# A fused sketch attention and tanh layer: the first batch's keys by groups, its products spread over more engines, and a newly searched order

## The chip, the cores and the metric

The kernel runs on one core of a Trainium2 chip. Its time is the device time of one execution in microseconds, and the median of several runs is what counts. The core has five engines with a queue of instructions each, which they take strictly in order: TensorE (PE in the profile, with its weight loads as PEld), VectorE (DVE), ScalarE (ACT), GpSimd (POOL) and SyncE (SP), which here only issues transfers. Engines wait for each other through semaphores. Work is in SBUF (128 partitions) and in PSUM (eight banks, where matmuls put their results).

## What is computed

Two stages behind each other. The first is attention with a polynomial sketch: keys and queries go through two small matrices S1 and S2, the two results are multiplied with each other in all 8 x 8 pairs, and attention is linear in these 64 products. The second adds a wide layer whose activation is h - tanh(h).

```python
# q, k, v: (4 batches, 4 heads, 1088 rows, 32); S1, S2: (8, 32)
def phi(x):
    a = einsum('rd,bhsd->bhsr', S1, x)
    b = einsum('rd,bhsd->bhsr', S2, x)
    return einsum('bhsi,bhsj->bhsij', a, b).reshape(..., 64)
q_p, k_p = phi(q), phi(k)
kv  = einsum('bhsf,bhsd->bhfd', k_p, v)
z   = sum(k_p, axis=2)
num = einsum('bhsf,bhfd->bhsd', q_p, kv)
den = einsum('bhsf,bhf->bhs', q_p, z)[..., None] + 1e-06
x   = (num / den) as (4352 tokens, 128)
h   = x @ w_in                # w_in: (128, 2048)
out = (h - tanh(h)) @ w_out   # w_out: (2048, 128)
```

The kernel splits the last line: x @ (w_in @ w_out) is done with one folded 128 x 128 matrix, and tanh(-h) @ w_out is added.

## The kernel before

The tokens are handled as four batches of 1088 rows, each of nine tiles of 128 (the last is half full). A batch's attention goes through these steps, named here as in the code:

- **kT**: the raw keys are turned on DVE in blocks of 32 x 32 (L595 in the first batch, L591 later). **kproj** (L604): PE projects them with the sketches (psk). **kab** (L612): DVE turns the projections back, into the two factors a and b per key.
- **gram** (L620): PE adds up a times b over all keys, which gives z. **zm** (L625), **ufold** (L629) and **uw** (L632) fold z into w4, the matrix that projects the queries.
- **qT** (L762), **qproj** (L774), **qab** (L782): the queries' turn, projection with w4, and turn back; the product with z comes out with them.
- **wk** (L652): the 64 products per key. In the first batch ACT first copies a part of kab into PSUM (**ka**, L641), so that DVE reads one operand there. **tiles** (L665, **sums** L734 in later batches): PE multiplies wk with v. **kvs**, **fold0** and **kvb** bring the result into the form that the numerators use.
- **dm**, **den**, **rden**, **qa** (L801 to L810): the denominator, its reciprocal, and the query factor divided by it. **qp** (L685, L820 later): the 64 products per query. In the first batch PE turns them (**qt0**, L700) and ACT or DVE copies them back (**qpB**, L707); in later batches DVE turns them (qpT, L826).
- **num** (L716, L843 later) and **x** (L722): the numerators, which are x.

The second stage goes through ten windows of tokens: 256, 256, seven of 512, and 256. A window has 16 matmuls of **L1** (L952, one for each block of 128 hidden columns), the **tanh** on ACT (L956), 16 of **L2** (L973), and two of **lin** (L937) with the folded matrix in two bf16 parts, whi and wlo. L1 writes two pairs of PSUM banks in turn, L2 and lin add in one bank; DVE turns the result (osb, L989) and SP writes it out. The last window multiplies the other way about (L968). Ahead of the dense part w_in and w_out are cast to bf16 (L872, L876), w_in is transposed on PE in four steps (**turn**, L886; copied by w_inT, L891), and **wfold** (L898) multiplies the two matrices.

The order of all this is not the code's. Each step is recorded as an operation with an engine, a cost, what it reads and writes, and a priority; ORDER lists for each engine the operations' numbers in the order in which they are issued, found by a search ahead of time, and PLACES gives for some steps another engine than the code names. Semaphore waits are worked out from the recorded reads and writes. Where PE would have nothing to do in the opening, matmuls of a tile of zeros (wz, L531 and L532) are put in; how many is worked out from the planner's costs.

The opening's queues before the change are these. SP issues k (three transfers: 160 columns of each of four groups, 128 of three groups, 64 of the last), q's first 512 columns, v (four), w_in and w_out, with the rest of q between. DVE turns the keys in two parts (five tiles, then four), then does kab of five tiles, qT, kab of four, qT, one wk, zm, a wk, uw, two wk, qab (two), dm, den, rden, qa (two of each), and four qp. POOL does wk of the first five tiles, then casts weights. PE does kproj in two parts, gram, ufold, qproj, tiles, fold0, qt0 of tiles 0 and 1 with two of w_in's transposes between, qt0 of tiles 2 and 3, the numerators, the third transpose, and then L1.

Of the kernel before, what the change touches and what calls it, by code (L numbers as in the profile page):

```python
# [13 lines left out]
R = 8  # L14
# [4 lines left out]
NT = 9  # L19
# [3 lines left out]
FB = 0  # L23
# [7 lines left out]
COLD = 6800  # L31
EARLY = 5000
CHUNK = 256
HEAD = 56
# [19 lines left out]
    ),  # L54
    "scalar": (
# [4 lines left out]
    ),  # L60
    "vector": (
# [5 lines left out]
    ),  # L67
    "gpsimd": (
        "4 15 17 16 2 3 25 5 20 19 21 77 75 18 76 102 103 107 104 24 106 146 148 23 238 237 22 243 247 360 359 361 370 366 502 "
        "503 504 509 513 "  # L70
    ),
    "sync": (
# [7 lines left out]
PLACES = {"qpB0.2": "scalar", "w_inT0": "scalar", "x0.2": "scalar", "cast_out1": "scalar", "qpB0.4": "scalar", "qpB0.6":  # L80
          "scalar", "x0.4": "scalar", "kvs3": "scalar", "w_inT1": "vector", "x0.1": "vector", "w_inT2":
          "vector", "x0.8": "vector", "kvw1": "vector", "kvs2": "vector", "cast_in3": "gpsimd", "cast_out2":
# [23 lines left out]
class Program:  # L106
# [13 lines left out]
    def op(self, eng, cost, fn, r=(), w=(), prio=0.0, sem=None, mode=None, name="", after=(), ni=2, two=False, alt=None):  # L120
# [5 lines left out]
        o.alt = alt  # L126
        for k in r:
# [17 lines left out]
        for k in r:  # L145
            if k not in w:
                self.readers.setdefault(k, []).append(o)
# [9 lines left out]
    def schedule(self):  # L157
# [21 lines left out]
        while left:  # L179
# [20 lines left out]
            if e == "tensor":  # L200
                if filling and o in self.fill_stops:
                    filling = False
                if filling and fills_from in order["vector"]:
                    free[e] = max(free[e], fills_from.at + fills_from.cost + 90, 990)
                    while True:
                        rate = 1.2 if free[e] < COLD else 2.4
                        wide = 512 if free[e] + 512 / rate + 60 <= o.at else 128
# [3 lines left out]
                        f = Op("tensor", long, self.filler[0 if wide == 512 else 2], 0, None, None, "fill")  # L211
# [12 lines left out]
                while passed // CHUNK > block:  # L224
                    block += 1
                    self.fetch.append((block, o.name, o.at, have[block] - o.at))
                    o.at = max(o.at, have[block])
                    have.append(o.at + (5800 if o.at < 24000 else 3500))
# [134 lines left out]
def bass_polysketch_attn__then__act_tanh_shrink_kernel(nc, q, k, v, S1, S2, moe_w_in, moe_w_out, out):  # L363
# [11 lines left out]
    def dve(n):  # L375
        return 75 + n / 0.96
# [58 lines left out]
    KG = 9 * 32  # L435

# [25 lines left out]
    def load_small():  # L462
        for i, src in enumerate((S1, S2)):
            o = load("scalar", 1024, ("s_raw",), "s", -1000, lambda e, i=i, src=src: e.dma_start(
                out=s_raw[8 * i:8 * i + 8, :], in_=src[:, :]), True)
            o.lag = 800 * i - 500
# [16 lines left out]
    def load_keys(prio):  # L483

        src = k[0].rearrange("h (j c) d -> (h j) (c d)", j=32)
        dst = kraw[0][:, :].rearrange("p (g f) -> p g f", f=KG)

        def runs(g0, g1, lo, hi):
            rows = src[:, KG * g0 + lo:KG * g0 + hi]
            rows = bass.AP(tensor=rows.tensor, offset=rows.offset, ap=[rows.ap[0], [KG, g1 - g0], rows.ap[1]])  # L490
            return lambda e: e.dma_start(out=dst[:, g0:g1, lo:hi], in_=rows)  # L491

        for x, (g0, g1, lo, hi) in enumerate(((0, 4, 0, 160), (0, 3, 160, 288), (3, 4, 160, 224))):
            size = 512 * (g1 - g0) * (hi - lo)
            o = load("sync", size, ("kraw0", min(x, 1)), f"k0{min(x, 1)}", prio, runs(g0, g1, lo, hi), x == 2, (350, 378, 100)[x])
            o.lag = (-200, 150, 150)[x]
            if x == 2:
                asked.append((o, size))
# [30 lines left out]
    def constants():  # L529
        wzero = P.op("vector", 150, lambda e: e.memset(wz[:, :], 0.0), w=[("wz",)], prio=-2000, name="wz")  # L530
        P.filler = (lambda e: e.matmul(ps[:, FB, 0:512], wz[:, :], wz[:, None, :].to_broadcast([128, 4, 128]), start=True, stop=True), wzero,  # L531
                    lambda e: e.matmul(ps[:, FB, 0:128], wz[:, :], wz[:, :], start=True, stop=True))  # L532
# [585 lines left out]
```

## Time and profile before

| | us |
|---|---|
| median of 3 runs | 105.68 |
| the runs | 104.93, 105.68, 105.86 |
| profiled execution, whole | 104.86 |
| its span in the trace | 102.6 |

The profiled execution is a run of its own, and stands a little below the lowest of the three. The span goes from the first to the last instruction in the trace; 2.26 us of the execution lie around it. A row of the timeline has the start, the time, the engine and line, the operation, what it writes and reads with the sizes, how many instructions are merged, and in brackets how long the engine was idle before it and what ended that. A row of the chain has the start, the time, and what it was. A matmul on four-byte floats counts as two PE instructions. Instructions of one engine overlap a little, so the distance from one start to the next says more than the time of one.

### The profile page before, as it was taken

To read this page: it belongs to the slowest core of one execution; us is meant where nothing else is said; L and a number is where in the kernel's file an instruction comes from. 1 tells how busy PE (TensorE), PEld (TensorE's weight loads), DVE (VectorE), ACT (ScalarE), POOL (GpSimd) and SP (SyncE) were. 2 spreads that over 40 slices of the span, in tenths; PEclk is the share of its full clock that TensorE was granted. 3 is DMA by queue.
4 is the path that set the end of the run, shared out by engine and by line. 5 is a ranking of instruction groups with operands and counts; after the bars stand their busy time and mean duration, and the time that the engine had idled before them with its cause. 6 is when DMAs were issued, how large, how long until landed. Compare 5 with 4: busy or idle time off the path is not lost.

```text
span 102.6 us, 3008 instructions
## 1 busy us (share of the span) xinstructions
PE 96.7 (94%) x1278; PEld 52.2 (51%) x1278; DVE 60.0 (58%) x129; ACT 79.2 (77%) x110; POOL 34.1 (33%) x43
## 2 busy tenths in 40 slices
PE   6969989999999999999999999999999999999970
PEld 2336747884676543434555343644444434445760
DVE  0778975997999897699678437837840020020120
ACT  3431768978767956787998797999869999999970
POOL 5347345420956800973910079083000000000000
PEclk9999999999999999999999999999999999999999
DMA  2999999910079804870003544030013611016254
GB/s 46 292 216 309 388 382 270 205 30 6 13 170 235 264 12 135 205 228 0 6 0 58 112 85 93 8 47 0 0 19 55 92 26 19 0 27 98 45 80 93
DMA packets 24029, 11.21 MB, mean 109 GB/s; under 512 B 18000, under 2 KB 21200, under 8 KB 24016
## 3 DMA queue, kind: packets, MB, share of 16 engines
q1 hardware_dynamic: 23840, 10.95, 44.2%
q8 instruction: 10, 0.16, 0.7%
q10 hardware_dynamic: 176, 0.07, 0.2%
q14 instruction: 3, 0.02, 0.1%
HBM read 8.78 MB, written 2.23 MB: 107 GB/s over the span
## 4 chain that ended last, share of the span: by engine, by line
PE 86%; DVE 5%; DMA 4%; SPq 1%; issue 0%
PE ps L952 31%; PE ps L973 27%; PE ps L843 4%; DMA qraw<-in_q_dram 4%; PE ps L937 4%; PE ps L734 3%; PE ps L774 3%; PE ps L716 2%; PE ps L604 2%; PE ps L700 2%; PE ps L968 2%; DVE qp L685 2%; SPq L491 1%; PE ps L620 1%; PE ps L898 1%; PE ps L629 1%
## 5 line engine op out<-in xcount | busy, mean ns | idle before, releaser
L956 ACT ACTIVATE tt<-ps 128x1024 bf16<-128x1024 f32 (+1 forms) x70 | 66.2, 998 | 8.0 <-PE ps L952 7.7
L952 PE MATMUL ps<-xT,w_in 128*128 128x512 bf16 (+1 forms) x160 | 42.7, 351 | 0.0
L973 PE MATMUL ps<-tt,w_out 128*128 128x512 bf16 (+1 forms) x144 | 38.2, 356 | 0.0
L952 PEld LDWEIGHTS ps<-xT,w_in 128*128 128x128 bf16 x160 | 16.3, 115 | 14.7 <-ACT tt L956 3.7
L652 POOL TENSOR_TENSOR wk<-kab 128x768 f32<-128x768 f32 (+2 forms) x11 | 15.5, 1405 | 21.0 <-DVE kab L612 20.4
L973 PEld LDWEIGHTS ps<-tt,w_out 128*128 128x128 bf16 x144 | 14.1, 99 | 11.9 <-issue 0.9
L989 DVE STREAM_TRANSPOSE osb<-ps 128x512 f32<-128x512 f32 (+1 forms) x9 | 5.9, 657 | 20.5 <-PE ps L973 20.3
L820 POOL TENSOR_TENSOR qp<-qa,qab 128x768 f32<-128x768 f32 x6 | 10.6, 1768 | 7.2 <-DVE qa L810 6.9
L826 DVE STREAM_TRANSPOSE qpT<-qp 128x768 f32<-128x768 f32 x9 | 8.6, 964 | 3.0 <-POOL qp L820 3.0
L782 DVE STREAM_TRANSPOSE qab<-ps 128x576 f32<-128x576 f32 (+2 forms) x10 | 6.0, 642 | 2.0 <-PE ps L774 1.7
L531 PE MATMUL ps<-wz 128*128 128x512 bf16 x14 | 5.7, 510 | 1.0 <-DVE wz L530 1.0
L762 DVE STREAM_TRANSPOSE qT<-qraw 128x576 f32<-128x576 f32 (+2 forms) x9 | 5.9, 657 | 0.2
L612 DVE STREAM_TRANSPOSE kab<-ps 128x576 f32<-128x576 f32 (+2 forms) x5 | 3.3, 654 | 2.7 <-PE ps L604 2.7
L843 PE MATMUL ps<-qpT,kvw 32*32 32x288 f32 (+1 forms) x192 | 4.6, 399 | 0.0
L591 DVE STREAM_TRANSPOSE kT<-kraw 128x576 f32<-128x576 f32 x6 | 4.5, 743 | 0.0
L855 ACT CAST xT<-ps 128x256 bf16<-128x256 f32 (+2 forms) x6 | 2.2, 373 | 2.4 <-PE ps L843 2.4
L734 PEld LDWEIGHTS ps<-wk,vx 128*32 128x32 f32 x216 | 3.2, 110 | 1.0 <-issue 0.6
L734 PE MATMUL ps<-wk,vx 128*32 128x64 f32 x216 | 3.6, 220 | 0.0
L700 PE MATMUL ps<-ident,qp 128*128 128x128 f32 (+1 forms) x18 | 3.1, 280 | 0.6 <-DVE qp L685 0.6
L707 ACT COPY qpB<-ps 128x512 f32<-128x512 f32 (+1 forms) x5 | 2.5, 500 | 1.4 <-PE ps L700 1.3
L843 PEld LDWEIGHTS ps<-qpT,kvw 32*32 32x32 f32 x192 | 2.4, 103 | 2.1 <-DVE qpT L826 0.5
L774 PE MATMUL ps<-qT,w 32*32 32x288 f32 (+2 forms) x160 | 3.4, 365 | 0.0
(99 smaller groups left out, 92.5 us busy)
## 6 DMA issues: line engine op xcount, KB each, us to landing
vx<-in_v_dram SPq DMA_DIRECT2D x12, 144.0 KB, 4.3
qraw<-in_q_dram SPq DMA_DIRECT2D x4, 288.0 KB, 5.2
qraw<-in_q_dram SPq DMA_DIRECT2D x4, 256.0 KB, 5.3
w_in_f<-in_moe_w_in_dram SPq DMA_DIRECT2D x4, 256.0 KB, 5.4
w_out_f<-in_moe_w_out_dram SPq DMA_DIRECT2D x4, 256.0 KB, 7.8
out_dram<-osb SPq DMA_DIRECT2D x16, 64.0 KB, 2.0
kraw<-in_k_dram SPq DMA_DIRECT2D x3, 288.0 KB, 4.4
kraw<-in_k_dram SPq DMA_DIRECT2D x3, 256.0 KB, 5.2
```

Of the source, the lines that this page charges most:

```text
L652: P.op(eng, dve(cols) if eng == "vector" else pool2(cols), lambda e, t0=t0, t1=t1, ap=ap, m=m, ka0=ka0: e.tensor_tensor(out=wk[:, t0:t1, : ...
L734: ins = e.matmul(ps[32 * h:32 * h + 32, vb, 0:64], vx[i][:, h, t, :], wk[:, t, h, :, :], start=(t == 0), stop=(t == NT - 1), tile_position ...
L762: P.op("vector", dve(hi - lo), lambda e: e.transpose(out=qT[i][:, lo:hi], in_=qraw[i][:, lo:hi]), r=cells("qraw", i, lo, hi), w=cells("qT" ...
L774: ins = e.matmul(ps[32 * g:32 * g + 32, qb + h, 0:n], w4[i][32 * h:32 * h + 32, :], qT[i][32 * h:32 * h + 32, :].rearrange("p (t g j) -> p ...
L782: P.op("vector", dve(2 * n), lambda e, h=h: e.transpose(out=qab[:, t0:t1, h:h + 2, :].rearrange("p t h x -> p h t x"), in_=ps[:, qb + h:qb ...
L820: P.op(eng, dve(cols) if eng == "vector" else pool2(cols), lambda e, p0=p0, p1=p1, w=w: e.tensor_tensor(out=qp[:, p0:p1, :, :, :].rearrang ...
L826: P.op("vector", dve(cols), lambda e, p0=p0, p1=p1: e.transpose(out=qpT[:, p0:p1, :, :, :].rearrange("p t h y j -> p (t h y j)"), in_=qp[: ...
L843: ins = e.matmul(ps[32 * h:32 * h + 32, nb[g], 0:32 * n], kvw[i][32 * g:32 * g + 32, y, 32 * h:32 * h + 32], qpT[32 * g:32 * g + 32, t0:t0 ...
L952: P.op("tensor", pe(n), lambda e, jb=jb + y, y=y, hb=hb: e.matmul(hb[:, n * y:n * y + n], hidden(w_in, jb), xT[:, f0:f0 + n], start=True, ...
L956: P.op("scalar", act(q * n), lambda e, un=un, hb=hb, q=q: e.activation(out=tt[:, un, 0:q * n], in_=hb[:, 0:q * n], func=AF.Tanh, scale=-1. ...
L973: P.op("tensor", pe(n), lambda e, jb=jb, un=un, y=y: e.matmul(acc[:, 0:n], w_out[:, jb, :], tt[:, un, n * y:n * y + n], start=(not f0 and ...
L989: P.op("vector", dve(n), lambda e: e.transpose(out=osb[u][:, 0:n], in_=acc[:, 0:n]), r=[ka], w=[("osb", u)], prio=slot0, name=f"osb{w}")
```

## The change

**Keys.** The first batch's keys come in four transfers, one for each group of 288 columns (the last with 224), instead of three that cut across the groups. DVE turns one group after the other, in the order 0, 1, 3, 2. PE projects them by pairs of groups and by two parts of the tiles, four operations in all; the order issued is groups 0 and 1 (first five tiles, last four), groups 2 and 3 (last four, first five). gram is two operations, for the first five tiles and the last four.

**Sketches.** The spread of the sketches over partitions was one operation of eight matmuls. It is now two: four matmuls for psk, and one matmul for the matrix that s2blk is made of. The copies of w4 are put behind psk and three of the s2blk on ACT.

**Products.** ka is copied for all nine tiles, in two parts and into two banks, and each wk of the first batch is one tile. More kinds of operation may now be put on another engine by PLACES. In the opening's list for POOL stand now, behind the constants: wk of tiles 2, 6 and 3, a memset, wk of tile 1, dm of tiles 0 and 1, wk of tile 8, the bf16 identity, qa of tiles 2 and 3, qp of tile 2, and then casts of weights. DVE has wk of tiles 0, 5, 7 and 4, dm of tiles 2 and 3, all den and rden, qa of tiles 0 and 1, and qp of tiles 0, 1 and 3. tiles is nine operations, in the order 0, 5, 1, 6, 2, 7, 3, 8, 4.

**L1.** In the first window each of the 16 matmuls of 256 columns is two of 128, each waiting for its own part of x. In PE's order the first of them stand behind all three numerators.

**Order.** All five lists are new, with some of the planner's constants. Beside what is said above: DVE does kab of the last four tiles, then of the first five, then the two qT, then zm. Of w_in's transposes, one stands ahead of the first L1 and three behind it (two stood ahead of the numerators, one ahead of L1, one behind). A cast of w_in and one of w_out stand on ACT ahead of the second and the third tanh. In later batches some wk, dm, qa, qp and copies change between DVE, POOL and ACT, and L1 and L2 are interleaved otherwise. PE has 21 zero matmuls instead of 26, of which five of 512 columns instead of six stand first.

```diff
-        for x, (g0, g1, lo, hi) in enumerate(((0, 4, 0, 160), (0, 3, 160, 288), (3, 4, 160, 224))):
-            size = 512 * (g1 - g0) * (hi - lo)
-            o = load("sync", size, ("kraw0", min(x, 1)), f"k0{min(x, 1)}", prio, runs(g0, g1, lo, hi), x == 2, (350, 378, 100)[x])
...
+        for g in range(4):
+            lo, hi = KG * g, min(KG * g + KG, S)
+            size = 512 * (hi - lo)
+            o = load("sync", size, ("kraw0", g), f"k0{g}", prio, lambda e, lo=lo, hi=hi: e.dma_start(
+                out=kraw[0][:, lo:hi], in_=src[:, lo:hi]), rate=280)
...
-            for h in range(H):
-                ins = e.matmul(ps[32 * h:32 * h + 32, 6, 64:96], e16[:, :, :].rearrange("p a b -> p (a b)")[:, 32 * h:32 * h + 32],
-                               s_raw[:, :], start=True, stop=True, tile_position=(0, 32 * h))
...
+        P.op("tensor", 220, lambda e: e.matmul(ps[:, 6, 64:96], e16[:, :, :].rearrange("p a b -> p (a b)"), s_raw[:, :], start=True, stop=True),
+             r=[("s_raw",), ("e16",)], w=[bank[6]], prio=-2900, mode="s", name="pse", ni=4)
...
+        for x, (lo, hi) in enumerate(KCUT if b else [(KG * g, KG * g + KG) for g in range(4)]):
+            P.op("vector", dve(hi - lo), lambda e, lo=lo, hi=hi: e.transpose(
+                out=kT[:, lo:hi], in_=kraw[i][:, lo:hi]), r=cells("kraw", i, lo, min(hi, S)) + ([] if b else [("kraw0", x)]) + ([("kraw0", i, "z")] if hi > S else []),
+                w=[("kT", x)], prio=T["kT"], after=gate, name=f"kT{b}{x}")
...
+            for g in (0, 2):
+                for x, (t0, t1) in enumerate(KPART):
+                    P.op("tensor", (290, 280)[x], project(g, g + 2, t0, t1, kb[x]), r=[("psk", 0), ("psk", 1), ("kT", g), ("kT", g + 1)],
...
+        for t0, t1 in ((0, NT),) if b else KPART:
+            P.op("tensor", 34 * (t1 - t0), gram(t0, t1), r=[("kab", i, t) for t in range(t0, t1)], w=[bank[gb]], prio=T["gram"] + 0.01 * t0,
...
+            for (e0, e1), kb in zip(KPART, pb):
+                P.op("scalar", act(32 * (e1 - e0)), lambda e, e0=e0, e1=e1, kb=kb: mover(e)(
+                    ps[:, kb, 32 * e0:32 * e1], kab[i][:, 0, e0:e1, :, :].rearrange("p t h x -> p (t h x)")),
...
+                both = {"vector": dve(256), "gpsimd": pool2(256)}
+                P.op(eng, both[eng], product, r=[("kab", i, t)], still=[bank[pb[t >= KPART[1][0]]]],
+                     w=[("wk", t)], prio=T["wk"], name=f"wk{b}.{t}", alt=both)
...
+                for o, m in ((0, n),) if f0 else ((0, n // 2), (n // 2, n // 2)):
+                    P.op("tensor", pe(m), lambda e, jb=jb + y, y=y, hb=hb, o=o, m=m: e.matmul(
+                        hb[:, n * y + o:n * y + o + m], hidden(w_in, jb), xT[:, f0 + o:f0 + o + m], start=True, stop=True),
...
-    summed = values_first(opening, 2, 3, [(0, 2), (5, 7), (2, 4), (7, 9), (4, 5)])
+    summed = values_first(opening, 2, 3, [(t, t + 1) for t in SUMMED])
```

`still` names a bank that an operation needs filled: it waits for the bank's writer, but not for readers of the bank on other engines. A wk on POOL names it as well, and so waits for the ka of its part, although it reads kab alone.

More of the change, by code (lines that the diff above doesn't have):

```diff
@@ L118, in __init__, with op @@
         self.fetch = []
-    def op(self, eng, cost, fn, r=(), w=(), prio=0.0, sem=None, mode=None, name="", after=(), ni=2, two=False, alt=None):
+    def op(self, eng, cost, fn, r=(), w=(), prio=0.0, sem=None, mode=None, name="", after=(), ni=2, two=False, alt=None, still=()):
         if alt and name in PLACES:
@@ L126, in op @@
         o.alt = alt
+        for k in still:
+            o.deps.update(self.writer.get(k, ()))
         for k in r:
@@ L144, in op @@
             self.readers[k] = []
-        for k in r:
+        for k in (*r, *still):
             if k not in w:
@@ L206, in schedule @@
                         rate = 1.2 if free[e] < COLD else 2.4
-                        wide = 512 if free[e] + 512 / rate + 60 <= o.at else 128
+                        wide = next((x for x in (512, 256) if free[e] + x / rate + 60 <= o.at), 128 if rate < 2 else 256)
                         long = wide / rate + (3 if rate > 2 else 0)
@@ L485, in load_keys @@
         src = k[0].rearrange("h (j c) d -> (h j) (c d)", j=32)
[L486 to L491, printed above, removed]
[L493 to L498 removed]
+        for g in range(4):
[3 more added lines that the diff above has]
+                out=kraw[0][:, lo:hi], in_=src[:, lo:hi]), rate=280)
+            o.lag = -650
     def load_v(b, prio):
@@ L647, in key_products @@
             m = 4 * (t1 - t0)
-            near = pb is not None and eng == "vector"
             ka0, keys = ap[:, 0, :, :], [("kab", i, t) for t in range(t0, t1)]
-            if near:
-                ka0, keys = ps[:, pb, 32 * (t0 - e0):32 * (t1 - e0)].rearrange("p (m x) -> p m x", x=R), keys + [bank[pb]]
             P.op(eng, dve(cols) if eng == "vector" else pool2(cols), lambda e, t0=t0, t1=t1, ap=ap, m=m, ka0=ka0: e.tensor_tensor(
@@ L655, in key_products @@
                 op=ALU.mult), r=keys, w=[("wk", t) for t in range(t0, t1)],
-                prio=T["wk"] + n * T["wkstep"], name=f"wk{b}.{t0}", two=not near)
+                prio=T["wk"] + n * T["wkstep"], name=f"wk{b}.{t0}", two=True, alt={"vector": dve(cols), "gpsimd": pool2(cols)})
     def values_first(T, vb, tb, tiled):
@@ L687, in products_first @@
             in1=qab[:, t, :, None, R:2 * R].to_broadcast([128, H, R, R]), op=ALU.mult),
-            r=[("qa", t), ("qab", t)] + ([bank[sb0]] if near is not None else []), w=[("qp", t)], prio=T["qp"], name=f"qp0.{t}", two=near is None)
+            r=[("qa", t), ("qab", t)] + ([bank[sb0]] if near is not None else []), w=[("qp", t)], prio=T["qp"], name=f"qp0.{t}", two=near is None,
+             alt={"vector": dve(256), "gpsimd": pool2(256)} if near is None else None)
     def numerators_first(T, groups, nb, xeng):
@@ L802, in denominators @@
             out=flat(dm)[:, :, 0:R], in0=flat(qab)[:, :, 0:R], in1=flat(qab)[:, :, 2 * R:3 * R], op=ALU.mult),
-            r=[("qab", t) for t in ts], w=[("dm", t) for t in ts], prio=T["den"], after=gate, name=f"dm{b}.{t0}", two=True)
+            r=[("qab", t) for t in ts], w=[("dm", t) for t in ts], prio=T["den"], after=gate, name=f"dm{b}.{t0}", two=True,
+             alt={"vector": dve(8 * m), "gpsimd": pool2(8 * m)})
         P.op("vector", dve(8 * m), lambda e: e.tensor_reduce(
@@ L812, in denominators @@
             r=[("qab", t) for t in ts] + [("rden", t) for t in ts], w=[("qa", t) for t in ts] + ([] if near is None else [bank[near]]),
-            prio=T["den"], name=f"qa{b}.{t0}", two=near is None)
+            prio=T["den"], name=f"qa{b}.{t0}", two=near is None,
+             alt={"vector": dve(8 * m), "gpsimd": pool2(8 * m)} if near is None else None)
         return {} if near is None else {t: spot[:, 4 * (t - t0):4 * (t - t0) + 4, :] for t in ts}
@@ L856, in numerators @@
                 xb[:, g, 0:late, :], ps[:, nb[g], 0:32 * late].rearrange("p (t j) -> p t j", j=32)),
-                r=[bank[nb[g]]], w=[("x", b, t, g) for t in range(late)], prio=T["x"], name=f"x{b}.{t0}.{g}")
+                r=[bank[nb[g]]], w=[("x", b, t, g) for t in range(late)], prio=T["x"], name=f"x{b}.{t0}.{g}",
+                alt=either(n) if g > 1 and b < B - 1 else None)
             if b == B - 1:
```

96 lines of the change are left out of this document (50 added, 46 removed), and 61 rows, old and new, of tables (ORDER, PLACES).

## The prediction

> **What bounds the kernel now.** I read the shares of busy time first, then the slices over time, the busy time by stretch, and the chain that ended last.
>
> ```profile
> span 102.6 us, 3008 instructions
> ...
> PE 96.7 (94%) x1278; PEld 52.2 (51%) x1278; DVE 60.0 (58%) x129; ACT 79.2 (77%) x110; POOL 34.1 (33%) x43
> ...
> PE   6969989999999999999999999999999999999970
> ```
>
> ```profile
> 15.70:25.00 9.30, 9.30 (x128) 6.55 (x126) 7.55 (x18) 8.50 (x13) 2.70 (x6) 1.00 0.56 128
> ...
> 85.00:98.00 13.00, 13.00 (x82) 7.39 (x81) 1.43 (x2) 12.48 (x14) 0.00 (x0) 1.00 0.24 37
> ```
>
> ```profile
> 13.55 0.66 PE ps L700 x4
> 14.20 1.33 PE ps L716 x12
> 15.53 0.35 PE ps L886 x4
> 15.88 0.44 PE ps L952 x4
> ...
> 17.14 0.93 PE ps L952 x7
> ...
> 18.62 0.89 PE ps L898 x16
> ...
> 98.40 1.10 PE ps L968 x18
> 99.52 0.29 DVE olast L982
> ```
>
> The columns of the stretches are PE, PEld, DVE, ACT and POOL busy time. From the seventh slice on PE stays at 9, and in both stretches it is busy all the time; the chain runs on PE from 15.53 to 99.52 with nothing between. So the kernel has two parts. Until about 15.5 us an opening, in which PE mostly waits or multiplies zeros; then 84 us in which PE is the bound, with ACT close behind at the end (12.48 of 13.00). The change can gain in two ways: start the dense part sooner, or put less into it. The opening's rows on DVE, PE and POOL:
>
> ```profile
> 3.85 1.61 DVE L595 STREAM_TRANSPOSE kT<-kraw 128x640 f32<-128x640 f32 x2 [0.17 <-DMA kraw<-in_k_dram]
> 5.91 0.52 DVE L612 STREAM_TRANSPOSE kab<-ps 128x320 f32<-128x320 f32 x1 [0.45 <-PE ps L604]
> 6.55 0.45 DVE L762 STREAM_TRANSPOSE qT<-qraw 128x256 f32<-128x256 f32 x1
> 6.92 0.41 DVE L612 STREAM_TRANSPOSE kab<-ps 128x256 f32<-128x256 f32 x1
> 7.25 0.40 DVE L762 STREAM_TRANSPOSE qT<-qraw 128x256 f32<-128x256 f32 x1
> ...
> 8.00 0.18 DVE L625 TENSOR_TENSOR zm<-ps,mask 128x32 f32<-128x32 f32 x1
> ...
> 9.68 0.78 DVE L782 STREAM_TRANSPOSE qab<-ps 128x256 f32<-128x256 f32 x2
> ...
> 10.77 0.36 DVE L804 TENSOR_REDUCE den<-dm 128x8 f32<-128x72 f32 x2
> ...
> 11.28 0.23 DVE L810 TENSOR_TENSOR ps<-qab,rden 128x64 f32<-128x64 f32 x1
> ...
> 12.67 0.83 DVE L685 TENSOR_TENSOR qp<-qa,qab 128x256 f32<-128x256 f32 x1
> ```
>
> ```profile
> 5.30 0.72 PE L604 MATMUL ps<-kT,psk 64*32 64x160 f32 x32
> ...
> 7.38 0.37 PE L620 MATMUL ps<-kab 128*32 128x32 f32 x18 [0.87 <-DVE kab L612]
> ...
> 8.33 0.38 PE L629 MATMUL ps<-zm,s2blk 128*128 128x32 f32 x2
> ```
>
> ```profile
> 0.74 1.55 SPq L491 DMA_DIRECT2D kraw<-in_k_dram  x3
> ...
> 2.33 4.19 DMA qraw<-in_q_dram
> ```
>
> Three things are to be seen. DVE takes its work in order: the second kab (6.92) stands behind a qT that waits for q, and q lands at 2.33 + 4.19 = 6.52. From qab (9.68) to the last qp (12.67 + 0.83 = 13.50) DVE works alone. The transposes L700 at 13.55 wait for that qp, and everything up to the dense part follows from them.
>
> **The change, part by part.**
>
> ```profile
> kraw<-in_k_dram SPq DMA_DIRECT2D x1, 32.0 KB, 2.9
> ```
>
> *Four key loads for three.* An issue on SP takes 1.55 / 3 = 0.52, so q and all behind it on SP's queue (v, the weights) are issued 0.52 later. q then lands between 6.52 (the same bytes are ahead of it) and 7.04. Today's last piece of k starts its issue at about 1.79 and lands at 4.69 (2.9). The new last one starts at 0.74 + 3 x 0.52 = 2.30: between 4.69, if bytes decide, and 5.20, if the issue does. I take 4.8, nearer the first, since the total of bytes is the same. v and the weights have cover: their first users stand behind qab.
>
> *Keys turned by group, projected by pairs, kab ahead of qT.* A turn of 288 columns is worked out as 0.44 (256 take 0.41, 320 take 0.52); the first three overlap the landing of the next piece. The last ends at 5.24, where today's end at 3.85 + 1.61 = 5.46. The projections end 5.30 + 0.72 - 5.46 = 0.56 after it: 5.80. The two kab follow at 5.90 and, 0.34 on, at 6.24, and end at 6.76; today the second ends at 7.33, because qT is between. Both Gram halves now wait for this end (the short kab is first, and PE takes the other half first), so the split in two itself brings nothing. Gram: 6.81 to 7.18. The two qT are next on DVE and hold up zm: they begin at 6.6, or when q lands, and zm comes two steps of 0.33 on, at 7.3 to 7.7. I take 7.5, where today has 8.00. qab keeps its distance of 1.68: 9.18, done at 9.96.
>
> *Sketches' spread in two parts.* One matmul replaces four and the scaled copies of w4 move behind the spread; psk is there before 5.24, so at most 0.1 is won ahead of the projections, under the wait for k. Zero.
>
> ```profile
> 6.51 0.63 POOL L652 TENSOR_TENSOR wk<-kab 128x256 f32<-128x256 f32 x1 [2.64 <-DVE kab L612]
> ...
> 7.22 1.07 POOL L652 TENSOR_TENSOR wk<-kab 128x512 f32<-128x512 f32 x1
> ```
>
> ```profile
> 2.47 0.29 POOL L554 CAST identb<-ident 128x128 bf16<-128x128 f32 x1
> ```
>
> ```profile
> 12.59 0.62 POOL L872 CAST w_in<-w_in_f 128x512 bf16<-128x512 f32 x1
> ```
>
> ```profile
> L685 DVE TENSOR_TENSOR qp<-qa,qab x5: 424/826/850, 12.2 to 20.5; 128x256 f32<-128x256 f32 x5
> ```
>
> *Work moved from DVE to POOL.* This is the step that decides. POOL now takes, in order: wk of tiles 2, 6, 3, a memset, wk of tile 1, dm of tiles 0 and 1, wk of tile 8, identb, qa of tiles 2 and 3, qp of tile 2. It starts only when ACT has copied kab into PSUM (ka, some 0.3 after 6.76): 7.2, against 6.51 today. A wk of one tile costs 0.63, and 0.71 to the next start (6.51 to 7.22). Four of them and 0.2 for the memset: 10.24. dm and qa (64 columns) have no POOL row. The line through 0.63 (256) and 1.07 (512) gives 0.30; the ends are 0.10, about a memset, and 0.63. I take 0.30, as both rows are the same operation. dm then ends at 10.54, and den on DVE starts at 10.64: only 0.13 ahead of today's 10.77, although qab is 0.5 ahead. Behind dm: wk of tile 8 from 10.61, identb 11.32, qa 11.68, qp 12.05 to 12.68. DVE's own qp of tile 3 runs against POOL's: alone this operation takes 0.42, beside POOL 0.83, and today the last one ends 13.50 - (12.59 + 0.62) = 0.29 after POOL's cast. So 12.97, and L700 starts at 13.02, 0.53 sooner.
>
> That has POOL never held up by DVE. Two DVE operations with both operands in SBUF fall into POOL's row, dm of tiles 2 and 3 and qa of tiles 0 and 1, 0.23 each. If POOL has to wait for both, it is 0.46 later. I count one: the opening gains 0.30. The ends: 0.93 gained (dm and qa at 0.10, nothing held up), 0.80 lost (0.63 each, both blocks, POOL's qp at 0.83 instead of 0.63: 0.66 + 0.46 + 0.20 on -0.53).
>
> The Trainium skill, page "SBUF — State Buffer", section "SBUF: two separate sides", says that DVE and GpSimd share one port pair as an exclusive lock for a whole instruction, when a DVE operation has two SBUF inputs and the GpSimd one reads SBUF. The 424 and 826 ns above agree with it. By that rule both blocks occur and the opening gains 0.07 only, which would make the time 105.9; by the uncontended rows it would gain 0.53 and make it 105.4.
>
> *From L700 to the dense part* the order is the same (L700, L716, first L1), and ACT has the same copies between. w_in's first transpose and cast have time to spare there. So the dense part begins 0.30 sooner.
>
> *What goes into the dense part.* The second transpose of w_in, which PE does today in the opening while it waits, now stands behind the first L1: +0.35 (15.53 row). L1 of the first window is cut into halves, 32 matmuls of 128 columns for 16 of 256. At 0.89 / 16 = 0.056 each, against 0.44 / 4 = 0.11, that is +0.03; at the 1.10 / 18 = 0.061 of L968 it is +0.2. I take 0.1. It brings nothing back: in PE's order the first half stands behind all three numerators, and by then both halves of x are there. The 7 L1 at 17.14 take 0.93 where 7 x 0.11 = 0.77 would do; the new order has other work there, so -0.16. Two weight casts move onto ACT ahead of the second and third tanh, while copies go from ACT to DVE; ACT had 0.8 free in that stretch, so zero.
>
> ```profile
> PEld ps L843 <- DVE qpT L826: 0.5, 1, 0.5
> ```
>
> *Later batches.* Products and denominators change places between DVE and POOL, and L1 and L2 are interleaved otherwise. One wait such as this 0.5 may come or go. I take zero, and keep +-0.5.
>
> *Sum:* -0.30 + 0.35 + 0.1 - 0.16 = -0.01. The profiled execution took 104.86 (span 102.6 and 2.26 around it) and stands 0.82 below the median of 105.68. The forecast is 105.6 on the median's scale.
>
> **Rivals.**
> 1. *The opening's gain arrives* (faster). POOL's small operations are short and nothing holds them: -0.93 + 0.29 in the dense part = -0.64, and the searched order removes one wait of 0.5 later: 104.5. For it: kab's end is really 0.57 sooner. Against it: POOL's row has no slack.
> 2. *POOL becomes the opening's bound* (slower). Place: from ka to qp of tile 2. At the upper ends it is 0.80 late, and with 0.29 more in the dense part the sum is +1.09: 106.8. It decides as soon as that row ends later than 13.2, when the opening no longer pays for the dense part's extra work. For it: 826 ns beside 424. Against it: dm and qa would have to cost what an operation of four times their columns costs.
> 3. *PE's clock rises later* (slower).
>
> ```profile
> 4.93 0.44 PE L531 MATMUL ps<-wz 128*128 128x512 bf16 x1
> ...
> 5.96 0.39 PE L531 MATMUL ps<-wz 128*128 128x512 bf16 x1
> 6.18 0.33 PE L532 MATMUL ps<-wz 128*128 128x128 bf16 x3
> ```
>
> The zero product of 5.96 gives way after 0.22, where earlier ones take 0.44, so the clock doubles between 4.9 and 6.0. The change has five instead of six zero products ahead of the sketches. If the doubling is missed there, the projections, the Gram and L629 run at half speed: between nothing and 0.72 + 0.37 + 0.38 = 1.47 more on the path. I take 1.2, as most of each is matmuls one behind the other: 106.8. Against it: the pause grows by 0.4 us only. The Trainium skill, page "TensorE: Matmul & The Clock Gate", Part 1, lets the clock rise after a busy window of about 3.4 us that runs free of the kernel's start. The trace's rise, 4 to 5 us after the first product, is within one to two such windows.
>
> **How the numbers follow.** Forecast, little changed (own range 104.7 to 106.4): 0.48. Rival 1: 0.27. Rival 2: 0.20. Rival 3: 0.05. Over 1% means below 104.62 or above 106.74; that is about what a measurement of this kernel can tell from no change. Rival 1 is the chance of faster, 0.27; rivals 2 and 3 of slower, 0.25; 0.48 stay. The range 104.2 to 106.9 reaches into both sides and leaves out the outer parts of rivals 1 and 2, together no more than 0.2.
>
> **What would show it.** The second kab ends near 6.8 and qab starts near 9.2. POOL's row from 7.2 to 12.7 has no gap over 0.1. den starts near 10.6, L700's third group near 13.2, L1 near 15.2. The dense part lasts some 0.3 longer than today's 84 us. Wrong: a qab not before 9.5 (q late), a POOL row past 13.2, or a dense part that differs by more than 0.5.

## The result, and the profile after

| | before | after |
|---|---|---|
| median (four runs each) | 105.65 | 106.91 |
| the runs | 104.93 to 105.86 | 106.66 to 106.99 |
| ratio, 95% interval | | 1.0124 (1.0080 to 1.0168) |
| profiled execution, whole | 104.86 | 106.66 |
| its span | 102.6 | 104.9 |

The change makes the kernel slower by 1.24%. The forecast was 105.6, and the range ended at 106.9, just short of the median. In the profile's page after, PE, whose work the prediction weighed, looks as before until the last slices:

```profile
span 104.9 us, 3023 instructions
...
PE 98.5 (94%) x1283; PEld 53.3 (51%) x1283; DVE 61.8 (59%) x128; ACT 77.8 (74%) x110; POOL 34.4 (33%) x49
...
PE   6999789999999999999999999999999999999930
```

```profile
15.70:25.00 9.30, 9.30 (x140) 7.02 (x144) 7.34 (x18) 7.36 (x13) 4.29 (x9) 1.00 0.48 125
...
85.00:98.00 13.00, 13.00 (x73) 6.88 (x72) 0.72 (x1) 12.12 (x14) 0.00 (x0) 1.00 0.28 43
```

Both stretches are still PE's, busy all the time. The span is 2.3 us longer, in three places: the start of the dense part, the dense part, and what follows PE's last product. The opening's timeline after, DVE first, then PE, then POOL:

```profile
5.38 0.48 DVE L594 STREAM_TRANSPOSE kT<-kraw 128x288 f32<-128x288 f32 x1 [0.51 <-DMA kraw<-in_k_dram]
...
6.64 1.05 DVE L620 STREAM_TRANSPOSE kab<-ps 128x256 f32<-128x256 f32 x2 [0.35 <-PE ps L602]
7.72 0.77 DVE L783 STREAM_TRANSPOSE qT<-qraw 128x256 f32<-128x256 f32 x2
8.43 0.19 DVE L637 TENSOR_TENSOR zm<-ps,mask 128x32 f32<-128x32 f32 x1
...
10.05 0.78 DVE L803 STREAM_TRANSPOSE qab<-ps 128x256 f32<-128x256 f32 x2
...
11.61 0.36 DVE L826 TENSOR_REDUCE den<-dm 128x8 f32<-128x72 f32 x2 [0.34 <-POOL dm L822]
```

```profile
4.91 2.19 PE L602 MATMUL ps<-kT,psk 64*32 64x160 f32 x32
7.03 1.04 PE L535 MATMUL ps<-wz 128*128 128x512 bf16 x3
...
14.16 0.63 PE L721 MATMUL ps<-ident,qp 128*128 128x128 f32 x4 [0.31 <-POOL qp L705]
...
16.05 0.30 PE L978 MATMUL ps<-xT,w_in 128*128 128x128 bf16 x2
```

```profile
8.10 2.10 POOL L660 TENSOR_TENSOR wk<-kab 128x256 f32<-128x256 f32 x3 [4.63 <-ACT ps L653]
...
11.26 0.32 POOL L822 TENSOR_TENSOR dm<-qab 128x64 f32<-128x64 f32 x1
...
12.78 0.30 POOL L832 TENSOR_TENSOR qa<-qab,rden 128x64 f32<-128x64 f32 x1
13.15 0.86 POOL L705 TENSOR_TENSOR qp<-qa,qab 128x256 f32<-128x256 f32 x1
```

The third group of transposes (L721 at 14.16) now waits for POOL's qp, not for DVE's. And the end, first of the kernel before, then after:

```profile
97.15 0.72 DVE L989 STREAM_TRANSPOSE osb<-ps 128x512 f32<-128x512 f32 x1 [6.83 <-PE ps L973]
...
97.89 1.95 SPq L994 DMA_DIRECT2D out_dram<-osb  x4
...
99.88 0.64 SPq L985 DMA_DIRECT2D out_dram<-olast  x1
```

```profile
98.45 0.72 DVE L1016 STREAM_TRANSPOSE osb<-ps 128x512 f32<-128x512 f32 x1 [7.74 <-DMA out_dram<-osb]
99.19 3.12 SPq L1021 DMA_DIRECT2D out_dram<-osb  x6
100.57 0.29 DVE L1009 COPY olast<-ps 128x128 f32<-128x128 f32 x1 [1.40 <-PE ps L995]
100.86 0.66 ACTq L1012 DMA_DIRECT2D out_dram<-olast  x1
102.36 0.65 SPq L1012 DMA_DIRECT2D out_dram<-olast  x1
```

Before, SP issues the last transfer at 99.88, right behind the last copy (99.52 + 0.29 = 99.81). After, the copy is done at 100.86 (ACT copies the other half at the same time and issues its transfer at once), but SP is still issuing six others, and comes to the last at 102.36: 1.50 us pass for nothing. Ahead of them DVE's copy of window 8 ends its wait on a transfer (in brackets: DMA), where before it waited for PE.

On PE's timeline the dense part of the kernel before starts here:

```profile
15.46 0.41 PE L886 MATMUL ps<-identb,w_in 128*128 128x128 bf16 x4
```

So from profile to profile it starts at 16.05 instead of 15.46, +0.59; it lasts to 100.57 instead of 99.52, so 84.52 for 84.06, +0.46; the remaining 1.2 is the end. But that is one execution against one, and before's was 0.8 below its median. What the parts cost on the median is for the experiments to say.

### The profile page after: what moved, and what is told of

It is laid out like the page before. It is cut to its first block, busy times and chain, and to the rows that moved or that the text cites. A ratio compares the mean times of both kernels' runs of the same rounds, so it can differ in the third digit from the quotient of the medians.

```text
span 104.9 us, 3023 instructions
## 1 busy us (share of the span) xinstructions
PE 98.5 (94%) x1283; PEld 53.3 (51%) x1283; DVE 61.8 (59%) x128; ACT 77.8 (74%) x110; POOL 34.4 (33%) x49
## 4 chain that ended last, share of the span: by engine, by line
PE 80%; POOL 9%; DVE 5%; issue 1%; ACT 1%; POOLq 0%
PE ps L978 27%; PE ps L1000 23%; PE ps L866 4%; PE ps L602 4%; POOL qp L843 4%; POOL wk L660 3%; PE ps L962 3%; PE ps L795 3%; PE ps L535 2%; PE ps L755 2%; PE ps L995 2%; PE ps L721 2%; PE ps L737 2%; DVE qab L803 1%; DVE qpT L849 1%
## 5 line engine op out<-in xcount | busy, mean ns | idle before, releaser
L978 PE MATMUL ps<-xT,w_in 128*128 128x512 bf16 (+2 forms) x176 | 42.2, 334 | 0.0
L1000 PE MATMUL ps<-tt,w_out 128*128 128x512 bf16 (+1 forms) x144 | 37.2, 355 | 0.0
L672 POOL TENSOR_TENSOR wk<-kab 128x768 f32<-128x768 f32 x7 | 11.4, 1632 | 19.0 <-DVE kab L620 18.7
L843 POOL TENSOR_TENSOR qp<-qa,qab 128x768 f32<-128x768 f32 x4 | 7.6, 1896 | 2.5 <-DVE qa L832 2.3
L843 DVE TENSOR_TENSOR qp<-qa,qab 128x768 f32<-128x768 f32 x5 | 6.5, 1308 | 0.0
L594 DVE STREAM_TRANSPOSE kT<-kraw 128x576 f32<-128x576 f32 (+1 forms) x10 | 6.1, 631 | 0.6 <-DMA kraw<-in_k_dram 0.5
L535 PE MATMUL ps<-wz 128*128 128x512 bf16 x12 | 4.9, 509 | 1.0 <-DVE hmask L544 1.0
L660 POOL TENSOR_TENSOR wk<-kab 128x256 f32<-128x256 f32 x5 | 3.1, 626 | 5.0 <-ACT ps L653 4.6
L602 PE MATMUL ps<-kT,psk 64*32 64x288 f32 (+2 forms) x80 | 4.3, 427 | 0.0
L705 POOL TENSOR_TENSOR qp<-qa,qab 128x256 f32<-128x256 f32 x4 | 3.0, 760 | 2.1 <-DVE qa L832 1.8
```

The source lines that it names most:

```text
L602: ins = e.matmul(ps[32 * g:32 * g + 32, kb[r], 0:32 * (t1 - t0)], psk[64 * r:64 * r + 64, :, :, :].rearrange("p a h i -> p (a h i)"), grou ...
L660: return e.tensor_tensor(out=wk[:, t, :, :, :], in0=a[:, :, :, None].to_broadcast([128, H, R, R]), in1=ap[:, 1, :, None, :].to_broadcast([ ...
L672: P.op(eng, dve(cols) if eng == "vector" else pool2(cols), lambda e, t0=t0, t1=t1, ap=ap, m=m, ka0=ka0: e.tensor_tensor(out=wk[:, t0:t1, : ...
L843: P.op(eng, dve(cols) if eng == "vector" else pool2(cols), lambda e, p0=p0, p1=p1, w=w: e.tensor_tensor(out=qp[:, p0:p1, :, :, :].rearrang ...
L978: P.op("tensor", pe(m), lambda e, jb=jb + y, y=y, hb=hb, o=o, m=m: e.matmul(hb[:, n * y + o:n * y + o + m], hidden(w_in, jb), xT[:, f0 + o ...
L1000: P.op("tensor", pe(n), lambda e, jb=jb, un=un, y=y: e.matmul(acc[:, 0:n], w_out[:, jb, :], tt[:, un, n * y:n * y + n], start=(not f0 and ...
```

## The experiments

Ratios are to the kernel before, run on the same chip in the same rounds, each with its 95% interval. Times in us from different experiments lie up to 0.2 apart for that reason alone: the kernel before had medians of 105.45 to 105.67. So experiments are compared by their ratios. Windows are counted from 0. Four theories, T1 to T4, are tried.

**T1: the output order.** Windows 6 and 8 share one buffer, 7 has the other, so DVE's copy of window 8 waits until window 6 has been written out. In SP's list the transfers of window 6 (645 to 648) and 7 (692 to 699) are mixed, and the first of window 8 (743) stands ahead of the last two of 7:

```diff
-  645 591 592 692 693 694 695 696 646 697 647 648 743 698 699 744 745 746 787
+  645 591 592 646 647 648 692 693 694 695 696 697 698 699 743 744 745 746 787
```

> The changed kernel with one thing altered: SyncE issues the last three output transfers of the sixth window ahead of those of the seventh, and the last two of the seventh ahead of those of the eighth, as the kernel before does. T1 (the order of the output transfers costs the end): VectorE's copy of the eighth window no longer waits for the sixth window's transfers; it starts some 0.3 us sooner, and four instead of six transfers follow it on SyncE, so the last transfer is issued at about 100.9 us instead of 102.36, when its data are ready: 1.46 us sooner, near 105.4. Rival (the loss is all in the opening and in TensorE's own work, and the order at the end moves nothing): 106.9 as the changed kernel, or at best 0.3 less.

105.74, ratio 1.0033 (0.9998 to 1.0069).

```profile
97.93 0.72 DVE L1016 STREAM_TRANSPOSE osb<-ps 128x512 f32<-128x512 f32 x1 [6.84 <-PE ps L1000]
...
98.67 1.94 SPq L1021 DMA_DIRECT2D out_dram<-osb  x4
...
100.95 0.29 DVE L1009 COPY olast<-ps 128x128 f32<-128x128 f32 x1 [2.31 <-PE ps L995]
...
101.27 0.65 SPq L1012 DMA_DIRECT2D out_dram<-olast  x1
```

DVE waits for PE again, four transfers follow, and the last goes out at 101.27, with its copy done at 100.95 + 0.29 = 101.24. The loss falls from 1.24% to 0.33%. Half of the edit:

```diff
-  ... 743 698 699 744 745 746 787
+  ... 698 699 743 744 745 746 787
```

> The changed kernel with half of that: only the last two transfers of the seventh window go ahead of the first of the eighth; the sixth window's stay where they are. T1, split: two transfers of 0.52 us each (3.12 us for six) leave the queue behind the last eviction, so 1.0 us is won, and the rest of the 1.46 (VectorE's wait for the sixth window's transfers) stays: near 105.9. If the wait of VectorE is what costs: near 106.9.

105.93, ratio 1.0032 (0.9998 to 1.0067): as good as the whole, though in its profile DVE's copy still waits for the transfer, until 99.07.

```profile
99.07 0.72 DVE L1016 STREAM_TRANSPOSE osb<-ps 128x512 f32<-128x512 f32 x1 [7.60 <-DMA out_dram<-osb]
...
101.33 0.29 DVE L1009 COPY olast<-ps 128x128 f32<-128x128 f32 x1 [1.55 <-PE ps L995]
...
101.81 0.64 SPq L1012 DMA_DIRECT2D out_dram<-olast  x1
```

The last transfer goes out 0.19 behind its copy (101.33 + 0.29 = 101.62). So it is the two transfers queued behind the late one that cost; what DVE's wait costs by itself is too small for these intervals. The reverse, in the kernel before:

```diff
-  615 562 662 663 616 617 618 664 665 666 667 668 669 713 714 715 716 757
+  615 562 662 663 664 665 666 616 667 617 618 713 668 669 714 715 716 757
```

> The kernel before with the output order of the changed kernel: the last three transfers of the sixth window stand behind the first of the seventh's, and the first of the eighth ahead of the last two of the seventh. T1: the order alone costs the end 1.0 to 1.4 us: 105.45 + 1.2 = 106.6. Rival (in the kernel before these windows are done sooner, so the order has slack there): 105.5 to 105.7.

107.31, ratio 1.0180 (1.0134 to 1.0226), more than expected. The same picture as after:

```profile
98.78 0.72 DVE L988 STREAM_TRANSPOSE osb<-ps 128x512 f32<-128x512 f32 x1 [7.84 <-DMA out_dram<-osb]
...
100.14 0.29 DVE L981 COPY olast<-ps 128x128 f32<-128x128 f32 x1 [0.65 <-PE ps L967]
...
102.52 0.65 SPq L984 DMA_DIRECT2D out_dram<-olast  x1
```

Here the last copy is done at 100.43 and its transfer goes out at 102.52, 2.09 later. T1 is shown from both sides: the order costs 0.9% in the changed kernel and 1.8% in the kernel before.

**T2: POOL's row.** The identity's cast (25) goes back to the start, dm of tiles 0 and 1 (108) to DVE:

```diff
-  POOL: 5 20 85 89 86 19 84 108 91 25 125 142 ...
+  POOL: 5 25 20 85 89 86 19 84 91 125 142 ...
-  DVE:  93 87 122 109 ...
+  DVE:  93 87 108 122 109 ...
```

> The changed kernel with GpSimd's row in the opening relieved: the cast of the unit matrix goes back to the start of the kernel, and dm of the first two tiles goes back to VectorE; the number of zero products is held. T2 (GpSimd's row bounds the opening): the row from ka to qp of tile 2 is shorter by 0.32 + 0.3 us and their gaps, qp of tile 2 ends near 13.3 instead of 14.01, the third transpose group of qp starts near 13.5 instead of 14.16, and the time falls by 0.5 to 0.7 us, to about 106.3. Rival (the row only fills slack, and late projections set the opening by way of qab, den and VectorE's own products): the third group moves by less than 0.15 and the time stays at 106.9.

106.93, ratio 1.0145 (1.0099 to 1.0192): nothing won. In the profile the row is relieved, though:

```profile
12.66 0.30 POOL L832 TENSOR_TENSOR qa<-qab,rden 128x64 f32<-128x64 f32 x1 [0.80 <-DVE rden L829]
13.03 0.63 POOL L705 TENSOR_TENSOR qp<-qa,qab 128x256 f32<-128x256 f32 x1
```

POOL now idles 0.80 for DVE's rden, and its qp takes 0.63. DVE was late itself (qab starts at 10.72), and PE was slow that time (next theory). The same edit on top of the output order:

> The changed kernel with the output transfers in the order of the kernel before, and besides with GpSimd's row relieved (cast of the unit matrix at the start, dm of the first two tiles on VectorE). With GpSimd relieved alone, nothing was won although its profile had the first L1 at 16.05 us with the clock's rise at 8.9 us, where the kernel with the old output order alone had 16.51 with a rise at 8.7. T2a (the row does bound the opening, and the faulty order at the end swallowed the gain): 0.4 us below the kernel with the old output order alone, near 105.3. T2b (the row is slack on the average over executions): 105.7, as that kernel.

105.49, ratio 1.0001 (0.9968 to 1.0034): 0.3% below e1, which the intervals don't separate. T2 is not shown by the times. The traces give it some support: from the start of qab to the first L1 it is 5.66 to 6.00 us in the five without this edit, and 5.33 to 5.50 in four of the six with it, 5.83 and 5.84 in the other two.

**T3: the clock of PE.** A zero product of 512 columns takes 0.61 us at the half clock and 0.39 at the full one (0.43 and 0.21 to the start of the next). Three of them stand behind the projections: together they take 1.46 us when all are slow, and 0.82 when all are fast. First, more of them ahead of the projections:

```diff
-  zero products ahead of kproj: 256, 128, 128, 128 columns
+  512, 512, 512
```

> The changed kernel with three zero products of 512 columns ahead of the projections in place of one of 256 and three of 128, as many of them before the projections as in the kernel before. T3 (the clock of TensorE rises later because the products ahead of it are small): the clock rises near 6.0 us again instead of 7.2, the projections end near 6.5 instead of 7.10, the second kab near 7.1 instead of 7.69; the time falls by up to 0.6 us where GpSimd's row, which starts with kab, sets the end of the opening: about 106.3. Rival (the rise has another cause): the projections start 0.6 us later, still slow, end near 7.4, and the time rises by 0.3 us.

106.66, ratio 1.0124 (1.0070 to 1.0177): no gain, and in the profile the projections end at 6.90, between the two forecasts. The edit also delays the projections to 5.66, and leaves the thin stretch of the sketches (matmuls that use a few rows or columns of PE only) as it is. So the second try makes that stretch shorter and doesn't run past 5.0 (with the output order of e1):

```diff
-  spread for s2blk: one matmul onto 128 partitions
+  four onto 32 each, side by side, as in the kernel before
-  zero products ahead of kproj: 256, 128, 128, 128 columns
+  512, 512, 128
```

> The changed kernel with the output transfers in the order of the kernel before, and besides with TensorE kept denser until the projections: the sketches' second spread is four narrow products again as before (0.27 us instead of 0.56), and two zero products of 512 columns and one of 128 stand in place of one of 256 and three of 128. In the profiles so far the zero products show the clock's rise at 5.1 us before and at 7.4 to 8.9 in five executions of the changed kernel and its variants. T3 (what comes ahead of the projections is too thin for the clock to rise in time): the rise comes 1 to 2 us sooner in most executions, the projections of the second pair take 0.6 instead of 1.2 us, and the time falls by 0.4 to 0.7, to 105.0 to 105.3. Rival (the rise is a matter of when the execution begins, whatever the kernel does): 105.7.

105.29, ratio 0.9965 (0.9936 to 0.9994); e1's interval lies just above it. Which of the two edits did it was not separated.

```profile
4.99 1.34 PE L602 MATMUL ps<-kT,psk 64*32 64x160 f32 x32
6.26 0.82 PE L535 MATMUL ps<-wz 128*128 128x512 bf16 x3
...
15.29 0.30 PE L978 MATMUL ps<-xT,w_in 128*128 128x128 bf16 x2
```

From the other side, the kernel before without the two zero products ahead of its projections:

```diff
-  zero products ahead of kproj: 512, 512 columns
+  none
```

> The kernel before without the two zero products of 512 columns that stand between the sketches and the projections (its outputs do not depend on them). T3 from the other side: with 2.74 us of wide products from 0.99 to 3.73 us and then only sketches up to 5.3, fewer executions have enough dense work in time; where the rise is missed it comes up to 3.4 us later and the projections, the Gram product and the fold of the denominators run at half speed. The median rises by 0.3 to 0.7, to 105.9 to 106.3, and the runs spread more widely upwards. Rival (those two products do nothing but fill): 105.6.

106.06, ratio 1.0057 (1.0023 to 1.0092). Two matmuls that compute nothing are worth 0.6%:

```profile
5.34 1.26 PE L604 MATMUL ps<-kT,psk 64*32 64x160 f32 x32 [0.69 <-ACT psk L557]
6.53 0.61 PE L531 MATMUL ps<-wz 128*128 128x512 bf16 x1
```

The projections take 1.26 instead of 0.72, and the zero product behind them 0.61 instead of 0.39; by the trace's record of the granted clock the full clock comes at 9.66 instead of 5.05. T3 is shown from both sides as a cost of what stands ahead of the projections; that the cost comes about by way of the clock rests on these profiles, one of each kernel.

**All three repairs.**

> All three repairs together: output order, GpSimd's row and denser work ahead of the projections. If T2a and T3 both hold, the gains add: 105.7 - 0.4 - 0.5 = 104.8, below the kernel before (105.45). If one of them takes the other's place on the path (GpSimd's row and the projections feed the same products): 105.2. If neither holds: 105.7.

104.56 over six runs, ratio 0.9906 (0.9880 to 0.9932).

> The version with all three repairs once more, unchanged. Its six runs gave 104.56 us (0.9906 of the kernel before), while the same kernel with L1 whole gave 105.39 over twelve, although the two are alike up to the first L1 and their profiles spend the same 84.6 us from there on. If the repairs' gain is stable: 104.4 to 104.8 again, a ratio of 0.99. If the six runs were lucky in what varies from execution to execution ahead of the first L1 (the clock's rise, the landing of the last key piece, which of VectorE and GpSimd gets its turn first): 105.0 to 105.4, a ratio of 0.995 to 0.998.

105.03 over twelve, ratio 0.9946 (0.9915 to 0.9978): the time just in the second case, the ratio between the two. This version beats both kernels, by 0.5 to 0.9% the kernel before. Both profiles, of one and the same kernel:

```profile
6.31 0.82 PE L535 MATMUL ps<-wz 128*128 128x512 bf16 x3
...
14.79 0.31 PE L978 MATMUL ps<-xT,w_in 128*128 128x128 bf16 x2
```

```profile
6.89 1.09 PE L535 MATMUL ps<-wz 128*128 128x512 bf16 x3
...
15.85 0.30 PE L978 MATMUL ps<-xT,w_in 128*128 128x128 bf16 x2
```

The dense part differs in its start by 1.06 us between two executions. The rise of the clock (from the traces' record of the granted clock) and the opening in all profiles of the changed kernel's kind:

| kernel | three zero products | full clock from | first L1 |
|---|---|---|---|
| after | 7.03, 1.04 long | 7.53 | 16.05 |
| e1_tail | 7.27, 1.46 | 8.68 | 16.51 |
| e1_tail8 | 7.74, 1.37 | 8.88 | 16.88 |
| e2_pool | 7.07, 1.46 | 8.9 | 16.05 |
| e3_zeros | 6.83, 1.08 | 7.39 | 16.14 |
| e5_tail_pool | 7.16, 1.43 | 8.43 | 16.13 |
| e6_tail_clock | 6.26, 0.82 | 5.24 | 15.29 |
| e7, e10 (repaired) | 6.31, 0.82; 6.67, 0.82 | 5.69; 6.18 | 14.79; 15.69 |
| e11, e12 (repaired) | 6.84, 1.46; 6.89, 1.09 | 9.55; 7.48 | 16.10; 15.85 |

All fast in three of five with the denser start, in none of six without it: by these few profiles, together with e6's time, the repair makes an early rise likelier, not certain.

**The rest of the change.** L1 of the first window whole again, on top of the repairs:

```diff
-  for o, m in ((0, n),) if f0 else ((0, n // 2), (n // 2, n // 2)):
+  for o, m in ((0, n),):
```

> The version with all three repairs, and the first window's L1 whole again: 16 products of 256 columns in place of 32 of 128. By the prediction's step on the dense part the split costs 0.03 to 0.2: from the first L1 to the last TensorE product 84.6 us falls to 84.4 to 84.55, and the time from 104.56 to about 104.45. Rival (the halves let the first tanh start sooner and so pay for themselves): no change or up to 0.2 more.

105.39, ratio 0.9982 (0.9946 to 1.0019). But its profile has the dense part from 15.69 to 100.31, 84.62 us, and e7 from 14.79 to 99.38, 84.59. So in the profiles the split costs nothing. The 0.90 that e10's dense part starts later comes from ahead of the first L1, where the two kernels are alike: qab starts at 9.85 for 9.39, and a pair of DVE operations takes 0.78 for 0.34 (last section). T4 is that four key transfers make the last piece late. Keys in two transfers, on top of the repairs:

```diff
-  for g in range(4):
-      lo, hi = KG * g, min(KG * g + KG, S)
+  for g in (0, 2):
+      lo, hi = KG * g, min(KG * g + 2 * KG, S)
```

> The version with all three repairs, and the first batch's keys loaded in two transfers (two groups each) instead of four; turned by group and projected by pairs as in the changed kernel. T4 (four transfers make the last piece late: the last turn starts at 4.9 to 6.1 us in the profiles so far, where 4.8 was reckoned): two transfers are issued in 0.9 us less, the last turn starts at 4.8 to 5.0 and the queries land sooner: 0.2 to 0.3 us less, 104.3. Rival (a piece of two groups lands as late as the fourth piece does, and two turns of 0.48 follow it instead of one): 0.2 to 0.5 more, 104.8 to 105.0.

105.67, ratio 1.0021 (0.9984 to 1.0058): no gain. The last turn ends at 5.67 (three turns from 4.47 take 1.20), against 5.62 in e7 and 5.72 in e12 (5.14 and 5.24, 0.48 each). T4 falls. Why the time is above e12's is open: the clock rose late in its profile (table), but a profile is one execution.

## Why the prediction was wrong

**The step that failed** is *Later batches* ("Products and denominators change places between DVE and POOL, and L1 and L2 are interleaved otherwise. [...] I take zero, and keep +-0.5"). It looked for waits of PE only. SP's list was new too, and was read at its beginning and not at its end. What the runs show in its place is a last transfer that stands behind others on SP: 0.9% of the time, 1.0 us (1.0124 less 1.0033); in the profile 1.50 us pass between the last copy and its transfer. It was no rival either. Without it the kernel is at 1.0033, 0.35 us above the kernel before, where the sum says -0.01: within the 1% of "little changed". That the rest comes out so close is in part luck. The dense part alone is 0.4 longer, so by this estimate, which e1's interval leaves open by 0.35 either way, the opening neither wins nor loses on the median, though most of its steps below were wrong.

*Four key loads.* The last turn was to start at 4.80 and starts at 5.38, in other profiles of these four loads at 5.1 to 6.1. Too early, and it isn't four loads against two that decides it (e11).

*Keys, projections, kab.* The projections were to end 0.56 after the last turn, and end 1.24 after it (7.10 against 5.86). 0.56 was taken from an execution whose clock was up. Even then (e6) it is 0.75: 4.99 + 1.34 = 6.33 against 5.10 + 0.48. The second kab ends at 7.69 for 6.76, qab starts at 10.05 for 9.18. That is past the 9.5 that was to be the sign of a late q, but q was not late: qT follows kab at 7.72 without a wait. kab ahead of qT brings what it should only where the clock is up: in e7 qab starts at 9.39, before at 9.68.

*Sketches.* "Zero" was wrong. One matmul in place of four is thinner and longer work ahead of the projections (0.63 us at L573 for 0.34), and with fewer zero products it makes the clock rise later; making both denser is worth 0.7% (1.0033 less 0.9965 in e6). Rival 3 had this, with a chance of 0.05 and the reason that the pause grows by 0.4 us only. By the trace there is no pause at all: PE's matmuls follow each other without a gap from 0.99 until after the rise at 7.53.

*POOL's row.* The prices were right: dm 0.32 and qa 0.30 for 0.30, wk 0.70 apart (three in 2.10). qp took 0.86 for 0.63 with DVE's qp beside it. The row starts at 8.10 for 7.2 because kab is late, and ends at 14.01 for 12.68, past the 13.2 that rival 2 gives as its point (12.68 + 0.53, where the opening gains nothing; the dense part's 0.29 is paid for only up to 12.9). So rival 2 occurred in this profile, but its time of 106.8 came about for another reason: relieving POOL alone won nothing (e2). A gain of the size of rival 1 comes only with POOL and clock repaired as well: the kernel is then at 0.9946 and 0.9906, 0.6 to 1.0 us below the kernel before, where rival 1 put it 1.1 below.

*Dense part.* +0.46 against +0.29. This is not one draw: the dense part lasts 84.03 to 84.07 us in the three traces of the kernel before's kind (before, e8, e9), and 84.44 to 84.69 in the eleven of the changed kind. The split of L1 is zero and not 0.1 (e10), so what remains lies with the transposes and the new interleaving; this was not taken apart. The start is a draw: e8, which has the opening of the kernel before, starts its dense part at 16.07, no sooner than the changed kernel at 16.05.

*Sum.* -0.01 on 105.68 is 105.67; the forecast was written as 105.6.

## What to carry to other kernels

When all queues are newly ordered, read the list of the output queue to its end, and ask of each transfer what stands behind it: one that waits for its data holds up all others, and the last one is the kernel's end. PE's opening is to be priced at the slow clock as well as at the fast one, and a part that "only" makes early work thinner can delay the rise. One profiled execution is one draw: where the opening varies by 1 us between executions of one kernel, compare several before a term of 0.3 is believed.

## What was unexpected of the hardware

The rise of the clock differs between executions of one kernel. It came at 5.69 and at 7.48 us in e7 and e12, in the kernel before at 5.05, and at 4.24 in e8, which has the same opening. The full clock then holds for 95.57 us in ten of the fourteen traces and for 98.99 in four: 3.42 us more, or one step. The Trainium skill, page "TensorE: Matmul & The Clock Gate", Part 1, gives a window of about 3.4 us that runs free of the kernel's start; the traces agree with it. That PE is busy all the time is not enough: in e2 its matmuls leave no gap from 0.99 us until the rise at 8.9, 7.9 us later, while the kernel before pauses for 0.22 (3.94 to 4.16) and has its rise 4.06 after its first product. That a window must hold a certain share of dense products is argued from this, e6 and e9, not measured.

The same two small operations on DVE cost 0.34 or 0.78, and it seems to depend on when they meet POOL's. e7, then e12, each with POOL's pair of wk beside it:

```profile
9.82 1.41 POOL L660 TENSOR_TENSOR wk<-kab 128x256 f32<-128x256 f32 x2
...
10.41 0.34 DVE L822 TENSOR_TENSOR dm<-qab 128x64 f32<-128x64 f32 x2
```

```profile
10.34 1.38 POOL L660 TENSOR_TENSOR wk<-kab 128x256 f32<-128x256 f32 x2
...
11.03 0.78 DVE L822 TENSOR_TENSOR dm<-qab 128x64 f32<-128x64 f32 x2
```

In e7 both dm are done by 10.75, about where POOL goes from one wk to the next, and POOL's second wk takes 0.71; in e12 the second dm takes 0.65 alone and ends at 11.81, just after POOL's second wk (11.72). The same operations, then, 0.44 apart by a matter of timing. The lock that the prediction cites from the Trainium skill, page "SBUF — State Buffer", section "SBUF: two separate sides", would do this. The 0.44 reaches the dense part: from the start of qab to the first L1 it is 5.33 to 5.40 us in the three traces where the pair takes 0.34 (e2, e7, e11), 5.50 with 0.51 (e5), and 5.83 and 5.84 with 0.78 (e12, e10). So e7's time of 104.56 has a share of luck in it.
